# Layout of the count indicators, shorter vector steps in two routing phases, and the routing's rank, in a chunked attention and two-stage expert kernel

## The chip, the cores and the metric
The program runs on one core of a Trainium2 chip. The metric is the device time of one execution in microseconds. Before the change three runs took 1070.49, 1070.74 and 1074.46 us; the median is 1070.74 us. In the profile PE is TensorE's matmul, PEld its weight load, DVE is VectorE, ACT ScalarE, POOL GpSimd and SP the queue that issues most DMAs.

## The reference
Three stages follow each other, on 3072 tokens of 512 values.

```python
# 1 attention: chunks of 32 queries see 16 keys to the left, 8 to the right, and 8 memory keys
a = softmax(scale * q_c @ k_full.T);  x = a @ v_full
# 2 dense layer
r = maximum(x @ w_in, 0);  x = (s * r * r + b) @ w_out
# 3 experts: each token to one of 8 experts, at most 384 tokens each
order = argsort(-(x @ w_gate).flatten())
for idx in order:                 # all (token, expert) pairs, best first
    tok, e = idx // E, idx % E
    if assigned[tok] >= 0 or counts[e] >= cap: continue
    assigned[tok] = e;  counts[e] += 1
for e in range(E):
    out[mask_e] = maximum(x[mask_e] @ w1[e], 0) @ w2[e]
```

The loop over pairs can't be run pair by pair. It is computed in 8 phases. In each, every free token names its best open expert; the kernel searches the value at which the first expert would be full, accepts the tokens above it, and closes that expert. Which expert closes in a phase is known on the chip only, and its weights are then loaded by that number.

## The kernel before
**Stages.** Attention and the dense layer run over 24 tiles of 128 tokens, two tiles in a group. The dense products take each float32 operand as a rounded high part and a remainder, three matmuls for one. The last products of the dense layer (`late_products`, L366, matmuls `o` of L346) are kept back, so that TensorE has work while the first phase of routing runs. When the last of them is done, the last tile leaves PSUM (L373), is stored to DRAM, and the first expert's tokens are gathered from there (L994), transposed (`px`, L1014), split in high part and remainder (`xgh`, `xgl`, L1005 to L1010), and go through the two expert layers (`pf` in `ffn1`, `pg` in `ffn2`).

**A routing phase** (`route`, L810) makes five searches, of 7, 7, 6, 6 and 6 bits. A search compares each token's value with 128 or 64 thresholds: the indicators, 1 or 0, one column of thresholds for each of the 24 token tiles. They are bf16 and lie in two halves of 12 tiles each (`HT = 12`); the table of thresholds has 6 columns alike (`TB = 6`). VectorE makes a half in one step (`indicate`, L737; for the first search of the first phase in blocks, L726). TensorE then counts: 24 matmuls `pc` (L832), one for each token tile, with the tile's 128 indicators as weights and the 8 columns `oh` as the moving operand, after one matmul with constants. VectorE forms a minimum and maximum (`fl`, L835), TensorE spreads it (`pb`, L838), VectorE subtracts the threshold found (L843), and the next search begins. After five searches come sums (`pt`), the closed expert's number (`ei`), the list of its tokens (`listing`, L906, with `po` and `pi`), and the next phase.

Names in the trace: the indicators have no buffer of their own but stand in reused ones, so that they appear as `vw` (and sources as `kwin`, `wk`, `kT`). VectorE's routing instructions all carry L582, and matmuls of the planned part L761.

**Order of the work.** From the first phase on, the order of instructions on TensorE, VectorE and ScalarE is written by a planner (`run`, L776; `choose`, L767). It keeps a clock per engine from fixed prices (`Timed`, L567; 0.047 us for a `pc` matmul). Each task is a generator that yields an engine, a wait and a rank; among tasks ready on an engine, the lowest rank goes first, then the earliest. Between two yields a task's instructions stand together. The main work (late products, then experts) fills TensorE wherever no task is due. On the chip an engine runs its instructions in this order and waits for semaphores.

**Weights of the experts.** Each expert has two halves (h even: first layer, odd: second layer), each half four parts of 512 KB. A part is loaded by SP into a ring of four buffers, rounded by ScalarE (`rounding`, L964), and the remainder is formed by VectorE (`second`, L972, `e<-raws,e` in the trace). Ranks: routing 1 in phases 0 and 1, then 3; weight parts 1 for the first two halves, then 2.

Of the kernel before, what the change touches and what calls it, by code (L numbers as in the profile page):

```python
# [9 lines left out]
F32 = mybir.dt.float32  # L10
F32R = mybir.dt.float32r
BF16 = mybir.dt.bfloat16
I32 = mybir.dt.int32
AF = mybir.ActivationFunctionType
ALU = mybir.AluOpType
# [3 lines left out]
P = 128  # L19
# [5 lines left out]
def kernel(ctx, tc, q, k, v, mem_k, mem_v, w_in, w_out, moe_s, moe_b,  # L25
# [523 lines left out]
    RB = ((25, 7), (18, 7), (12, 6), (6, 6), (0, 6))  # L549
    NR = len(RB)  # L550
    T = NTILE
    NH = 2
    HT = T // NH
    TB = HT // 2
# [30 lines left out]
    V = Timed()  # L585
# [30 lines left out]
    sp = b0 = Pool()  # L616
# [22 lines left out]
    tabs, steps = [], []  # L639
    for r, (sh, nb) in enumerate(RB):  # L640
        n, lo = 2 ** nb, -2.0 ** 31 if r == 0 else 0.0
# [37 lines left out]
    def bt(x, n=T):  # L679
        return x[:, :, None].to_broadcast([P, x.shape[1], n])  # L680

    def be(x):
        return x[:, None, :].to_broadcast([P, E, T])
# [4 lines left out]
    def small(shape, dt, name):  # L688
        return sp.tile(shape, dt, tag=name, name=name)
# [1 line left out]
    ids, eid = {}, {}  # L691

    def indicators(n):
        return [sp.tile([P, P, HT], BF16, tag=f"ind{g}", name=f"ind{n}_{g}") for g in range(NH)]

    part = {}

    def prep(ph, t0, t1=T):

        n = t1 - t0  # L700
        if ph not in part:
            part[ph] = [small([P, E, T], F32, "Lm"), small([P, T], F32, "m"), small([P, T], I32, "sg"),
                        small([P, NR, T], I32, "di"), small([P, E, T], BF16, "eq"), small([P, T], BF16, "mw"),
                        small([P, E, T], BF16, "oh"), sp.tile([P, T], BF16, tag="de", name=f"de{ph}", bufs=2),
                        indicators(f"{ph}_0") if ph < E - 1 else None]
        Lm, m, sg, di, eq, mw, oh, de, ind = part[ph]
        Lz, mz, gz, dz, qz, wz, oz, ez = (x[..., t0:t1] for x in (Lm, m, sg, di, eq, mw, oh, de))

        def bn(x):
            return x[:, None, :].to_broadcast([P, E, n])  # L710

        V.tensor_tensor(Lz, L[:, :, t0:t1], bt(shut, n), op=ALU.add)
        V.tensor_reduce(mz, Lz.rearrange("p e t -> p t e"), axis=AX.X, op=ALU.max)
        yield
        V.tensor_tensor(qz, Lz, bn(mz), op=ALU.is_equal)
        V.tensor_tensor(qz, qz, bt(w8, n), op=ALU.mult)
        V.tensor_reduce(wz, qz.rearrange("p e t -> p t e"), axis=AX.X, op=ALU.max)
        V.tensor_tensor(oz, qz, bn(wz), op=ALU.is_equal)
        yield
        if ph < E - 1:  # L720
            mi = mz.bitcast(I32)
            V.tensor_scalar(gz, mi, 31, 2 ** 31 - 1, op0=ALU.arith_shift_right, op1=ALU.bitwise_and)
            V.tensor_tensor(gz, gz, mi, op=ALU.bitwise_xor)
            V.tensor_tensor(dz, gz[:, None, :].to_broadcast([P, NR, n]), masks[:, :, t0:t1], op=ALU.bitwise_and)
            V.tensor_tensor(ez, dz[:, 0, :], act[:, t0:t1], op=ALU.min)
            if ph == 0:  # L726
                for a in range(t0 - t0 % TB, t1, TB):
                    g, a, b = a // HT, max(a, t0), min(a + TB, t1)
                    V.tensor_tensor(ind[g][:, :2 ** RB[0][1], a - g * HT:b - g * HT],
                                    de[:, None, a:b].to_broadcast([P, 2 ** RB[0][1], b - a]),  # L730
                                    tabs[0][:, :, a % TB:a % TB + b - a], op=ALU.is_ge)
            for g in range(NH) if ph else ():
                if g:
                    yield
                indicate(ind[g], de, g, 0)

    def indicate(ind, de, g, r):  # L737
        n, z = 2 ** RB[r][1], [P, 2 ** RB[r][1], HT // TB, TB]
        V.tensor_tensor(ind[:, :n, :].rearrange("p n (a b) -> p n a b", b=TB),
                        de[:, g * HT:(g + 1) * HT].rearrange("p (a b) -> p a b", b=TB)[:, None].to_broadcast(z),  # L740
                        tabs[r][:, :, None, :].to_broadcast(z), op=ALU.is_ge)

# [2 lines left out]
    V_PE, PE_V, PE_A, A_V = 0.13, 0.19, 0.33, 0.06  # L747
# [11 lines left out]
    def matmul(cost, *args, **kw):  # L759
        clk["pe"] += cost  # L760
        return nc.tensor.matmul(*args, **kw)  # L761
# [45 lines left out]
    def slack(ph):  # L807
        return 0.1 if ph < 2 else 0.4

    def route(ph):  # L810

        rank = 1 if ph < 2 else 3
        sl = slack(ph)
        yield "v", 0.0, rank
        for _ in prep(ph, 0 if ph else T - GT):
# [1 line left out]
        oh, di, de, ind = (part[ph][i] for i in (6, 3, 7, 8))  # L819
        os = [small([P, E, T], BF16, f"os{i}") for i in range(2)]  # L820
        if ph < E - 1:
            for r in range(NR):
                ind = ind if r == 0 else indicators(f"{ph}_{r}")
                for g in range(NH) if r else ():
                    if g == NH // 2 and ph > 0:
                        yield "v", 0.0, rank
                    indicate(ind[g], de, g, r)
                yield "pe", V_PE - 0.5 + sl, 0
                pc = psa[0].tile([P, E], F32, tag="pa", name=f"pc{ph}_{r}")
                matmul(0.05, pc, first, q2, start=True, stop=False)  # L830
                for t in range(T):
                    matmul(0.047, pc, ind[t // HT][:, :, t % HT], oh[:, :, t], start=False, stop=(t == T - 1))  # L832
                yield "v", PE_V, 0
                fl = small([P, E], BF16, "fl")
                V.tensor_tensor_scan(fl, pc, ones[:, 0:E], 0.0, op0=ALU.max, op1=ALU.min)  # L835
                yield "pe", V_PE + sl / 2, 0
                pb = psa[0].tile([P, 2], F32, tag="pa", name=f"pb{ph}_{r}")
                matmul(0.05, pb, steps[r], fl[:, E - 2:E], start=True, stop=True)  # L838
                c = pb[:, 1:2]
                yield "v", PE_V, rank  # L840
                if r < NR - 1:
                    dn = sp.tile([P, T], BF16, tag="de", name=f"de{ph}_{r}", bufs=2)
                    V.scalar_tensor_tensor(dn, de, c, di[:, r + 1, :], op0=ALU.subtract, op1=ALU.add)  # L843
                    de = dn
            V.scalar_tensor_tensor(os[1], be(de), c, oh, op0=ALU.is_equal, op1=ALU.mult)
            pin = small([P, E, T], BF16, "pin")
            V.tensor_tensor_scan(flat(pin), flat(cont), flat(os[1]), 0.0, op0=ALU.mult, op1=ALU.add)
            V.scalar_tensor_tensor(os[0], be(de), c, oh, op0=ALU.is_gt, op1=ALU.mult)
            row = small([P, E], BF16, "row")
            with nc.allow_low_precision("counts of at most 24"):  # L850
                V.tensor_reduce(row, os[0], axis=AX.X, op=ALU.add)
            yield "pe", V_PE + sl, 0
            pt = psa[0].tile([P, 3 * E], F32, tag="pa", name=f"pt{ph}")
            matmul(0.05, pt[:, 0:E], ones, row, start=True, stop=True)
            matmul(0.05, pt[:, E:2 * E], ones, pin[:, :, T - 1], start=True, stop=True)
            matmul(0.05, pt[:, 2 * E:3 * E], tri, pin[:, :, T - 1], start=True, stop=True)
            yield "v", PE_V, rank
            need = small([P, E], F32, "need")
            V.tensor_tensor(need, rem, pt[:, 0:E], op=ALU.subtract)
            take = small([P, E], F32, "take")  # L860
            V.tensor_tensor(take, need, pt[:, E:2 * E], op=ALU.min)
            V.tensor_tensor(rem, need, take, op=ALU.subtract)
        else:
            V.scalar_tensor_tensor(os[0], be(act), 0.0, oh, op0=ALU.is_gt, op1=ALU.mult)
            V.memset(rem, 0.0)
# [21 lines left out]
        a = sp.tile([P, T], BF16, tag="a", name=f"a{ph}", bufs=2)  # L887
# [76 lines left out]
    def rounding(h):  # L964

        ph, half = divmod(h, 2)
        ws = [bigw([FT2, DM] if half else [KD, F2], f"e{half}{ph}_{a}") for a in range(2)]
        EW[ph] += ws
        rank = 1 if h < 2 else 2
        left = [NP]  # L970

        def second(hi, lo, raw):  # L972
            yield "v", A_V, rank
            V.tensor_tensor(lo, raw, hi.bitcast(F32), op=ALU.subtract)
            parted[0] += 1
            left[0] -= 1
            if not left[0]:
                loaded.add(h)

        for i in range(NP):  # L980
            while (h, i) not in raws:
                yield "a", 0.4, rank
            raw, at = raws[h, i]
            yield "a", 0.0 if h < 3 or i == 0 else 0.5, rank, at
            hi, lo = (w[part_of(h, i)] for w in ws)
            scalar(hi, raw, AF.Copy)
            new(second(hi, lo, raw), "a")
# [205 lines left out]
```

## Time and profile before
| | |
|---|---|
| median of three runs | 1070.74 us |
| the profiled execution | 1072.39 us |
| its span, first to last instruction | 1070.6 us |
| mean granted clock of TensorE | 0.984 |
| PE busy | 1010.0 us, 94% |
| DVE busy | 793.8 us, 74% |
| ACT busy | 460.7 us, 43% |
| POOL busy | 204.7 us, 19% |
| HBM read, written | 82.33 MB, 12.60 MB |

Busy times are sums over an engine's instructions; ends of matmuls are modelled and overlap, so the distance from one start to the next says more than a duration. [...] Routing and experts lie between about 683 us and the end.

### The profile page before, as it was taken

Reading aid. Unit: us, or ns where it says so; the run is one execution under the profiler, and the core shown is the slowest. Engines: PE = TensorE matmul, PEld = TensorE weight load, DVE = VectorE, ACT = ScalarE, POOL = GpSimd, SP = SyncE. Lnnn points to the kernel's source line nnn. Section 1 sums busy time; section 2 is a strip of 40 time slices with the busy share of each in tenths; the row PEclk is TensorE's granted clock in tenths of the full one; section 3 lists DMA queues with packets and bytes.
Section 4 is the critical chain, followed back from the end, with each engine's and each line's share of the span. In section 5 each row is a group of like instructions: output and inputs, shape, how many; then the busy total and the mean of one; then the engine's idle time right before and its main releaser. Section 6 shows DMA issues by size and latency. Waiting matters only on the chain.

```text
span 1070.6 us, 24583 instructions
## 1 busy us (share of the span) xinstructions
PE 1010.0 (94%) x9397; PEld 888.7 (83%) x9397; DVE 793.8 (74%) x2879; ACT 460.7 (43%) x991; POOL 204.7 (19%) x227
## 2 busy tenths in 40 slices
PE   4668899999999999999999999987999999999997
PEld 3647688888988889888888889866898988988996
DVE  4999864986698969898969854376968769678720
ACT  3666554444444544445444445312414334233621
POOL 2566540000021101021101000001103202032211
PEclk9989999999999999999999999996999999999999
DMA  6966504221212121212121100032624426235600
GB/s 158 230 184 185 148 19 128 58 58 38 58 38 59 39 58 38 57 39 59 38 58 39 38 2 2 20 117 91 197 92 145 130 88 208 88 140 176 227 30 30
DMA packets 140373, 96.52 MB, mean 90 GB/s; under 512 B 99288, under 2 KB 123864, under 8 KB 140128
## 3 DMA queue, kind: packets, MB, share of 16 engines
q1 hardware_dynamic: 135968, 81.32, 27.1%
q0 software_dynamic: 4000, 13.11, 3.4%
q8 instruction: 74, 1.21, 0.5%
q10 hardware_dynamic: 288, 0.52, 0.1%
q14 instruction: 43, 0.35, 0.1%
HBM read 82.33 MB, written 12.60 MB: 89 GB/s over the span
## 4 chain that ended last, share of the span: by engine, by line
PE 72%; DVE 14%; issue 6%; DMA 4%; ACT 1%; POOL 1%; SPq 1%; POOLq 0%; DVEq 0%; ACTq 0%
PE o L346 20%; PE ph L316 20%; PE pf L761 11%; PE pg L761 9%; DVE lsc L387 5%; PE pc L761 5%; DVE u L280 2%; DVE y L281 1%; DVE g L325 1%; PE po L221 1%; DMA xg<-x2d,vw 1%; PE sc L195 1%; PE px L1014 1%; DMA raw<-in_moe_w_out_dram 1%; DMA k<-in_k_dram 1%
## 5 line engine op out<-in xcount | busy, mean ns | idle before, releaser
L316 PE MATMUL ph<-xT,win 128*128 128x256 f32 x2304 | 321.9, 288 | 9.7 <-ACT win L262 6.9
L316 PEld LDWEIGHTS ph<-xT,win 128*128 128x128 f32 x2304 | 300.0, 192 | 27.5 <-ACT win L262 10.3
L346 PE MATMUL o<-wout,g 128*128 128x512 f32 x1038 | 275.3, 401 | 5.2 <-DVE g L325 2.2
L346 PEld LDWEIGHTS o<-wout,g 128*128 128x128 f32 x1038 | 185.1, 190 | 39.7 <-DVE g L325 3.1
L387 DVE SCALAR_TENSOR_TENSOR lsc<-x,wgb 128x128 int8<-128x128 f32 x640 | 158.2, 298 | 3.3 <-DMA wgb<-wgd 1.2
L320 ACT ACTIVATE r<-ph 128x256 f32<-128x256 f32 x192 | 72.7, 381 | 166.5 <-PE ph L316 155.8
L761 PE MATMUL pf<-xgh,e 128*128 128x384 f32 x512 | 137.9, 345 | 0.0
L761 PE MATMUL pg<-e,hh 128*128 128x512 f32 x384 | 124.3, 399 | 0.0
L325 DVE TENSOR_TENSOR g<-r,g 128x256 fp32r<-128x256 f32 x173 | 80.7, 468 | 53.3 <-ACT g L324 50.5
L387 DVE SCALAR_TENSOR_TENSOR lsc<-c,wgb 128x512 int8<-128x512 f32 x128 | 99.1, 774 | 2.1
L761 PEld LDWEIGHTS pf<-xgh,e 128*128 128x128 f32 x512 | 94.0, 192 | 0.4 <-ACT xgh L765 0.2
L761 PE MATMUL pf<-xgl,e 128*128 128x384 f32 x256 | 88.3, 345 | 0.3 <-DVE xgl L582 0.3
L765 ACT ACTIVATE hh<-pf 128x384 fp32r<-128x384 f32 x64 | 31.5, 492 | 129.1 <-PE pf L761 87.0
L765 ACT ACTIVATE e<-raws 128x1024 fp32r<-128x1024 f32 x64 | 65.7, 1056 | 45.5 <-DMA raws<-in_moe_w_dram 45.4
L321 ACT ACTIVATE r<-r 128x256 f32<-128x256 f32 x192 | 79.6, 417 | 5.5
L761 PEld LDWEIGHTS pg<-e,hh 128*128 128x128 f32 x384 | 71.1, 189 | 12.5
L582 DVE TENSOR_TENSOR e<-raws,e 128x1024 fp32r<-128x1024 f32 x64 | 76.8, 1218 | 3.9 <-ACT e L765 3.0
L761 PE MATMUL pg<-e,hl 128*128 128x512 f32 x192 | 75.8, 395 | 0.0
L324 ACT ACTIVATE g<-r 128x256 fp32r<-128x256 f32 x173 | 71.7, 417 | 5.0 <-PE o L346 0.3
L994 POOL DMA_INDIRECT xg<-x2d,vw x24 | 34.8, 1451 | 151.8 <-issue 118.2
L761 PE MATMUL pc<-kwin,vw 128*128 128x8 bf16 x840 | 56.2, 204 | 7.3 <-DVE vw L582 7.3
L582 DVE SCALAR_TENSOR_TENSOR hl<-pf,hh 128x384 fp32r<-128x384 f32 x64 | 35.1, 551 | 35.6 <-ACT hh L765 35.6
(171 smaller groups left out, 1276.7 us busy)
## 6 DMA issues: line engine op xcount, KB each, us to landing
raws<-in_moe_w_dram SPq DMA_DIRECT2D x64, 512.0 KB
vw<-in_v_dram SPq DMA_DIRECT2D x176, 56.0 KB
raw<-in_moe_w_in_dram SPq DMA_DIRECT2D x16, 512.0 KB
raw<-in_moe_w_out_dram SPq DMA_DIRECT2D x16, 512.0 KB
k<-in_k_dram SPq DMA_DIRECT2D x24, 256.0 KB
q<-in_q_dram SPq DMA_DIRECT2D x24, 256.0 KB
x2d<-x SPq DMA_DIRECT2D x20, 256.0 KB
wgb<-wgd SPq DMA_DIRECT2D x1, 2048.0 KB
```

Source lines behind the costliest of these rows:

```text
L280: nc.vector.scalar_tensor_tensor(u, yi, 3, u, op0=ALU.logical_shift_left, op1=ALU.bitwise_or)
L316: nc.tensor.matmul(ph, win_ap(a, kk, f), x[:, kk, :], start=(n == 0), stop=(n == 3 * KD - 1))
L320: nc.scalar.activation(r, ph, AF.Relu)
L321: nc.scalar.activation(r, r, AF.Square)
L324: nc.scalar.activation(hi, r, AF.Copy)
L325: nc.vector.tensor_tensor(lo, r, hi.bitcast(F32), op=ALU.subtract)
L346: nc.tensor.matmul(PO[j][u], g[:, u * P:(u + 1) * P], wout_ap(a, f), start=(f == 0 and n == 0), stop=(f == FT - 1 and n == 2))
L387: nc.vector.scalar_tensor_tensor(sc[:, z], a[:, z], 1.0, b[:, z], op0=ALU.mult, op1=ALU.mult, accum_out=acc[:, i:i + 1])
L582: return getattr(nc.vector, name)(out, *args, **kw)
L761: return nc.tensor.matmul(*args, **kw)
L765: nc.scalar.activation(out, in_, func)
L994: nc.gpsimd.indirect_dma_start(out=xg[:, j, :], out_offset=None, in_=x2d[:, :], in_offset=bass.IndirectOffsetOnAxis(ap=ids[ph][:, j:j + 1] ...
```

## The change
The change edits four places.

1. The indicators' layout. Each half is now two blocks of six token tiles; in a block the thresholds are the outer and the six tiles the inner index. Neighbouring thresholds of one tile stand 6 elements apart instead of 12. `indicate` writes both blocks of a half in one step as before, with the axes in the new order.
2. In phases 0 and 1 the indicators are made block by block (768 or 384 elements a step, no longer 1536 or 768); in the first search of phase 1 the planner may put other work between the blocks.
3. `second` forms the remainder of a weight part in two steps for the first three halves, and other work may come between.
4. Routing has rank 2 instead of 3 from phase 2 on, the same as weight parts.

```diff
     def indicators(n):
-        return [sp.tile([P, P, HT], BF16, tag=f"ind{g}", name=f"ind{n}_{g}") for g in range(NH)]
+        return [sp.tile([P, HT // TB, P * TB], BF16, tag=f"ind{g}", name=f"ind{n}_{g}")
+                .rearrange("p k (n b) -> p k n b", b=TB) for g in range(NH)]
...
-            if ph == 0:
-                for a in range(t0 - t0 % TB, t1, TB):
-                    g, a, b = a // HT, max(a, t0), min(a + TB, t1)
-                    V.tensor_tensor(ind[g][:, :2 ** RB[0][1], a - g * HT:b - g * HT],
-                                    de[:, None, a:b].to_broadcast([P, 2 ** RB[0][1], b - a]),
-                                    tabs[0][:, :, a % TB:a % TB + b - a], op=ALU.is_ge)
-            for g in range(NH) if ph else ():
+            for a in range(t0 - t0 % TB, t1, TB) if ph < 2 else ():
+                if ph and a:
+                    yield
+                a, b = max(a, t0), min(a - a % TB + TB, t1)
+                V.tensor_tensor(ind[a // HT][:, a % HT // TB, :2 ** RB[0][1], a % TB:a % TB + b - a],
+                                de[:, None, a:b].to_broadcast([P, 2 ** RB[0][1], b - a]),
+                                tabs[0][:, :, a % TB:a % TB + b - a], op=ALU.is_ge)
+            for g in range(NH) if ph > 1 else ():
                 if g:
                     yield
                 indicate(ind[g], de, g, 0)
 
     def indicate(ind, de, g, r):
-        n, z = 2 ** RB[r][1], [P, 2 ** RB[r][1], HT // TB, TB]
-        V.tensor_tensor(ind[:, :n, :].rearrange("p n (a b) -> p n a b", b=TB),
-                        de[:, g * HT:(g + 1) * HT].rearrange("p (a b) -> p a b", b=TB)[:, None].to_broadcast(z),
-                        tabs[r][:, :, None, :].to_broadcast(z), op=ALU.is_ge)
+        n, k = 2 ** RB[r][1], HT // TB
+        z = [P, k, n, TB]
+        V.tensor_tensor(ind[:, :, :n, :],
+                        de[:, g * HT:(g + 1) * HT].rearrange("p (a b) -> p a b", b=TB)[:, :, None, :].to_broadcast(z),
+                        tabs[r][:, None, :, :].to_broadcast(z), op=ALU.is_ge)
...
-        rank = 1 if ph < 2 else 3
+        rank = 1 if ph < 2 else 2
...
-                    indicate(ind[g], de, g, r)
+                    if ph > 1:
+                        indicate(ind[g], de, g, r)
+                    else:
+                        n = 2 ** RB[r][1]
+                        for k in range(HT // TB):
+                            V.tensor_tensor(ind[g][:, k, :n, :], de[:, None, g * HT + k * TB:g * HT + (k + 1) * TB]
+                                            .to_broadcast([P, n, TB]), tabs[r], op=ALU.is_ge)
...
-                    matmul(0.047, pc, ind[t // HT][:, :, t % HT], oh[:, :, t], start=False, stop=(t == T - 1))
+                    matmul(0.047, pc, ind[t // HT][:, t % HT // TB, :, t % TB], oh[:, :, t], start=False, stop=(t == T - 1))
...
         def second(hi, lo, raw):
-            yield "v", A_V, rank
-            V.tensor_tensor(lo, raw, hi.bitcast(F32), op=ALU.subtract)
+            m = raw.shape[1]
+            k = m // 2 if h < 3 else m
+            for z in range(0, m, k):
+                yield "v", A_V if z == 0 else 0.0, rank
+                V.tensor_tensor(lo[:, z:z + k], raw[:, z:z + k], hi[:, z:z + k].bitcast(F32), op=ALU.subtract)
```

## Rows read from the trace of the kernel before
**Rows 1.** The page: engine, busy us (share of the span), instructions.
```profile
PE 1010.0 (94%) x9397; PEld 888.7 (83%) x9397; DVE 793.8 (74%) x2879; ACT 460.7 (43%) x991; POOL 204.7 (19%) x227
```
**Rows 2.** Windows: stretch, its us, busy us per engine (instructions), PEclk, DMA, GB/s.
```profile
685.00:715.00 30.00, 30.00 (x230) 23.95 (x229) 18.79 (x59) 2.12 (x2) 0.74 (x1) 1.00 0.27 90
710.00:745.00 35.00, 23.45 (x186) 19.91 (x184) 25.95 (x52) 10.61 (x13) 5.71 (x4) 0.66 0.44 145
860.00:903.60 43.60, 43.60 (x319) 38.55 (x318) 34.23 (x83) 15.31 (x24) 8.53 (x6) 1.00 0.40 135
745.00:1055.00 310.00, 309.92 (x2072) 276.41 (x2071) 220.08 (x512) 110.28 (x169) 56.68 (x43) 1.00 0.40 131
```
**Rows 3.** The chain of waits, expert layers without other work: start, us, what.
```profile
759.55 5.49 PE pg L761 x24
...
996.29 16.67 PE pf L761 x96
```
**Rows 4.** The tile `pc`, and two of its streams in the timeline.
```profile
L761 PE MATMUL pc<-kwin,vw x840: 188/204/232, 685.4 to 966.2; 128*128 128x8 bf16 x168
...
693.41 1.61 PE L761 MATMUL pc<-kwin,vw 128*128 128x8 bf16 x24
...
900.41 1.58 PE L761 MATMUL pc<-kwin,vw 128*128 128x8 bf16 x24
```
**Rows 5.** The timeline: first of three matmuls with contiguous bf16 weights, and their successor.
```profile
882.60 0.18 PE L761 MATMUL pt<-wk,kT 128*128 128x8 bf16 x1
...
882.69 0.42 PE L761 MATMUL pf<-xgl,e 128*128 128x384 f32 x1
```
**Rows 6.** Half a stream at the lower clock: its window and its matmuls.
```profile
723.75:724.75 1.00, 0.89 (x12) 0.80 (x12) 1.00 (x2) 0.84 (x1) 0.95 (x1) 0.50 1.06 320
...
723.81 0.89 PE L761 MATMUL pc<-kwin,vw 128*128 128x8 bf16 x12 [2.08 <-DVE vw L582]
```
**Rows 7.** VectorE's indicator steps: groups (busy us, mean ns), two in the timeline.
```profile
L582 DVE TENSOR_TENSOR vw<-vw,wk 128x1536 bf16<-128x1536 bf16 x8 | 7.5, 953 | 0.1
L582 DVE TENSOR_TENSOR vw<-vw,wk 128x768 bf16<-128x768 bf16 x14 | 7.3, 554 | 0.2
L582 DVE TENSOR_TENSOR vw<-kwin,kT 128x256 bf16<-128x256 bf16 x1 | 0.4, 402 | 0.0
692.60 1.02 DVE L582 TENSOR_TENSOR vw<-kwin,kT 128x768 bf16<-128x768 bf16 x2
```
**Rows 8.** The chain between second stage and first expert (first row: timeline).
```profile
716.64 0.96 DVE L582 TENSOR_TENSOR vw<-vw,kT 128x1536 bf16<-128x1536 bf16 x1
...
717.51 0.74 DVE x L373
...
723.80 7.66 DMA xg<-x2d,vw
...
732.62 1.45 PE pc L761 x25
...
734.41 0.88 ACT xgh L765 x2
...
735.33 1.94 DVE xgl L582 x4
...
738.08 1.63 PE pc L761 x24
```
**Rows 9.** Weight remainders (group), and the timeline before one expert's first layer.
```profile
L582 DVE TENSOR_TENSOR e<-raws,e 128x1024 fp32r<-128x1024 f32 x64 | 76.8, 1218 | 3.9 <-ACT e L765 3.0 <-PE pf L761 0.9
...
899.25 0.95 DVE L582 TENSOR_TENSOR vw<-vw,kT 128x1536 bf16<-128x1536 bf16 x1
900.12 1.22 DVE L582 TENSOR_TENSOR e<-raws,e 128x1024 fp32r<-128x1024 f32 x1
906.67 0.55 DVE L582 TENSOR_TENSOR xgl<-px,xgh 128x384 fp32r<-128x384 f32 x1
911.45 0.34 PE L761 MATMUL pf<-xgh,e 128*128 128x384 f32 x1
```

## Prediction
> **What bounds the kernel now.** I read the page first: TensorE is busy for 94% of the span, VectorE for 74% [rows 1]. A share alone does not say that TensorE is the limit, so I read the windows next [rows 2]: the reader is to see that from 745 to 1055 us TensorE is busy for 309.92 of 310.00 us, and for all of a stretch of 43.60 us, which is one expert with one phase of routing. Busy could still hide slow issue, so I looked at how the matmuls of an undisturbed expert follow each other: 96 of the first layer take 16.67 us, or 174 ns for 384 columns, and 24 of the second take 5.49 us, or 229 ns for 512 [rows 3]. Both are 0.45 ns per column, so the columns set the pace and not the issue, and these 33.1 us per expert stay. What is left of the 43.60 us is mostly counting: one count is a stream of 25 matmuls with 8 columns each, which holds TensorE for 1.45 us (one of them on the chain [rows 8]), five times per expert, 7.3 us or 17%.
>
> In this half of the kernel TensorE has real idle time only between 710 and 745 us, 35.00 - 23.45 = 11.55 us [rows 2]. There the chain of waits leaves TensorE: it runs through the step of VectorE that takes the second stage's last tile out of PSUM (717.51), its store, the gather (7.66 us of DMA), the transposes and the subtractions to the first expert [rows 8].
>
> **Term 1: the weight load of a count.** The tile loads 128 weights per matmul, bf16. Before, neighbouring weights stand 12 elements (24 bytes) apart; after, 6 elements (12 bytes). The number of matmuls stays: 7 phases of 5 searches over 24 tiles, 840 [rows 4]. In the stream that starts at 693.41, 24 matmuls take 1.61 us, the last alone 0.204 us, so one follows the other after (1.61 - 0.20)/23 = 61 ns; other streams give 60. Three matmuls of the same shape with contiguous weights, the group pt, begin at 882.60, and the next matmul at 882.69: 30 ns each [rows 5]. So the step costs a factor of two, though it is twelve times the contiguous one: it looks like a step in the cost and not a slope. [...]
>
> No row has weights 12 bytes apart. The bounds are the two rows: 60 ns (no gain) and 30 ns (all of it). A loss I exclude, because the step moves toward the cheap row. Twelve is 10 bytes from the contiguous row and 12 from the strided one; a line drawn between them would give 44 ns. Since the ratio of two looks like a threshold I take 35 ns, near the contiguous row, and keep 44 as a case of its own. Saving: 24 x (60 - 35) = 0.60 us per stream, at the ends 0 and 0.72.
>
> [...]
>
> How many streams lie on the path? Between 685 and 715 us TensorE never waits, since products of the second stage fill every gap (30.00 us of 30.00 [rows 2]); a shorter stream ends that stage sooner: 5. In the idle stretch the first two streams of the second phase run while the gather is awaited and gain nothing; the third, 1.45 us from 732.62, stands on the chain in front of the last transposes [rows 8]. From it on all do: 3 of the second phase, 25 of the five after it. 33 x 0.60 = 19.8 us. This needs that nothing else takes over. Per expert VectorE has 34.23 us of work, DMA 0.40 of its time [rows 2]; at 40.6 us per expert VectorE would be at 84%.
>
> **Term 2: short steps in the first two phases.** One indicator step becomes two. From two steps in a row (1.02 us for two of 554 ns, so a pitch of 0.47 us for 768 elements; 0.953 against 0.554 us for 1536 and 768) a step costs 0.52 ns per element and 0.07 us beside [rows 7]. Two steps more per search are 0.14 us; 4 searches of the first phase and 5 of the second, 1.3 us of VectorE. In the first phase VectorE is busy for 18.79 us of 30.00 [rows 2] and TensorE is full, so it is covered; were that cover gone it would cost 4 x 0.14 = 0.6 us. Inside a stream a block lasts 0.5 us against 0.2 for its six matmuls, but the stream starts when three blocks are done, as before. In the second phase TensorE once waits for such a step (the stream at 738.08 comes straight behind one [rows 8]); I take +0.5 us in all. In return the store of the last tile, which started at 717.51 behind an indicator step of 0.96 us begun at 716.64 [rows 8], meets a step of half that: -0.4 us (0 to -0.9).
>
> **Term 3: halved remainders of the first three weight halves.** 12 subtractions of 1.218 us [rows 9] become 24 of some 0.65, about 0.7 us more of VectorE in all, while TensorE waits for the gather. At 735.33 the four subtractions on the chain start behind one of them; their own input was ready near 734.9 [rows 8], so -0.4 us (0 to -0.4).
>
> **Term 4: the routing's rank.** From the third phase on a routing step no longer yields to a weight part, the earlier ready one goes first. No work is added. It is queued in VectorE's order before later weight parts; behind these wait the matmuls of the next expert, and on SP the load of the part four later, which needs the same buffer. How much room is there? In one expert the last part of the first layer's weights starts at 900.12 and lasts 1.22 us, the last remainder of the gathered rows at 906.67, and the layer starts at 911.45 [rows 9]. That leaves the weights 10.1 us and the gathered rows 4.2 us. Routing's long steps in that stretch are four of 0.95 us, one of them between two parts [rows 9]; even all four, 3.8 us, cost the weights nothing, and the routing gains what they lose. Because TensorE now reaches each point sooner while VectorE's order is made with an unchanged price per count, I add +1.0 us for short waits (0 to 4).
>
> **Sum.** -19.8 + 0.5 - 0.4 - 0.4 + 1.0 = -19.1 us. From the profiled execution (1072.39 us, span 1070.6) that is 1053.3; the median of the runs lies 1.65 us below that execution, so 1051.6. I forecast 1052; this case's own range is 1046 to 1057 (30 ns and no waits; 38 ns and 4 us of waits).
>
> **Rivals.**
> *No gain from the step (chance 0.18).* If the quick load depends on weights that lie side by side, any gap costs the same, the stream stays at 60 ns, and terms 2 to 4 leave -0.3 to +0.7: 1070. For it: the only fast row is contiguous, and the two levels of the cost may have their step anywhere between 2 and 24 bytes. Against it: nothing in the trace but that 12 lies midway. [...]
> *Part of the gain (0.13).* If the cost is a slope after all, the line between the two rows gives 44 ns, 0.38 us per stream and 33 x 0.38 = 12.7 us; with the other terms 1059. For it: no row excludes a slope. Against it: 24 bytes cost only twice what 2 cost. [...]
> *Slower (0.07).* The indicator step walks its axes in a new order. A step of another walk, 256 elements in pairs, took 402 ns [rows 7], (0.402 - 0.155, what 554 ns leave beside 768 elements)/256 = 0.96 ns per element against 0.52. If the new order falls to that rate, a step of 1536 takes 0.7 us longer and one of 768 0.35. The second half of each of the first two searches then comes after the stream needs it: for the stream at 900.41 [rows 4] the second step, begun at 899.25 [rows 9], would end near 901.6 instead of 900.2 and is wanted at 901.1; with the next search 0.7 us per phase in five phases. The routing grows by 4 x 0.7 + 6 x 0.35 = 4.9 us per phase, over the 4.2 us that the gathered rows have: 0.7 in six phases. With streams at 60 ns that is +7.7: 1078. It decides from a step of about 1.4 us. Against it: both orders have runs of 6 elements, and such steps run at 0.52 ns now.
>
> **From cases to numbers.** Forecast case 0.62. A change below 0.5% (5.4 us) cannot be told from none here. Faster: the forecast and the part gain, 0.75. Same: 0.18. Slower: 0.07. The range runs from 1045 (33 x 0.72 us, and no waits) to 1069, taking in the part gain and the near end of no gain.
>
> **What would show it.** A count's stream of 25 matmuls at about 0.9 us instead of 1.46; steps of VectorE at unchanged 0.95 and 0.55 us; two experts 40.6 us apart instead of 43.6; the stretch without TensorE work after the second stage beginning 3 us sooner and as long as before. A stream at 1.4 us would prove term 1, and with it the forecast, wrong. A stream at 0.9 with experts still 43 us apart would mean that VectorE's or the routing's chain had become the limit: then TensorE shows idle time before the first layer.

## The result and the profile after

The changed kernel takes 1058.76 us (three runs, 1058.63 to 1059.53), the kernel before 1070.74: 12.0 us less by these medians. The ratio of the runs is 0.9876 [0.9853, 0.9900], which would be 13.3 us: the kernel before varied from 1069.4 to 1075.2 us between executions, and beside run 5 below it stood 12.9 us higher. The forecast was 1052 and the range 1045 to 1069. The profiled execution took 1058.63 us, 13.8 less than the one of before (1072.39).

The page of the changed kernel, in the columns of [rows 1]: TensorE is 12.2 us less busy with the same number of instructions, VectorE does as much as before.

```profile
PE 997.8 (94%) x9397; PEld 876.6 (83%) x9397; DVE 793.6 (75%) x2909; ACT 460.4 (44%) x991; POOL 202.1 (19%) x227
```

The counts come first. These are the tile `pc`, a stream of it in the timeline (start, us; the matmul with constants stands apart), and two entries of the chain of waits with that matmul (start, us, what):

```profile
L764 PE MATMUL pc<-kwin,vw x840: 177/190/213, 685.5 to 950.7; 128*128 128x8 bf16 x168
```

```profile
700.27 1.27 PE L764 MATMUL pc<-kwin,vw 128*128 128x8 bf16 x24
```

```profile
700.39 1.15 PE pc L764 x25
...
726.08 1.11 PE pc L764 x25
```

The median duration of one `pc` went only from 204 to 190 ns [rows 4], but they overlap; what matters is the distance between starts. 24 matmuls took 1.61 us [rows 4] and take 1.27: (1.27 - 0.19)/23 = 47 ns from one to the next, by the chain (1.15 - 0.04)/24 = 46, where it was 60. A stream of 25 holds TensorE for 1.15 us instead of 1.46 (1.45 in [rows 8]). The second of the two entries lies in a stretch where the granted clock is 0.50, half of full speed, and takes no longer (1.11 us).

Windows of the changed kernel, in the columns of [rows 2]; the third and fourth stretch are one expert with one phase each, from the start of one expert's first count to that of the next:

```profile
685.00:715.00 30.00, 29.40 (x233) 22.89 (x231) 19.99 (x69) 2.20 (x3) 0.74 (x1) 1.00 0.28 95
710.00:745.00 35.00, 24.96 (x213) 22.41 (x212) 28.92 (x75) 11.49 (x16) 4.40 (x4) 0.76 0.42 139
845.32:887.60 42.28, 42.28 (x323) 37.23 (x321) 34.18 (x83) 15.92 (x24) 8.97 (x7) 1.00 0.41 136
887.60:929.39 41.79, 41.79 (x320) 36.67 (x319) 34.08 (x83) 14.54 (x23) 7.27 (x7) 1.00 0.42 140
735.00:745.00 10.00, 10.00 (x94) 9.36 (x93) 7.39 (x20) 1.61 (x4) 0.00 (x0) 0.98 0.01 2
```

An expert takes 42.28 and 41.79 us, on average 42.03 instead of 43.60 [rows 2]: 1.57 us less, which is 5 streams x 0.31 us. TensorE stays busy throughout, so nothing else has become the limit. The last row belongs to the idle stretch; the same ten microseconds of the kernel before read:

```profile
735.00:745.00 10.00, 9.25 (x71) 7.90 (x69) 5.63 (x14) 1.55 (x4) 0.00 (x0) 0.61 0.00 0
```

Its granted clock there was 0.61 and is 0.98. At 0.50 (731 to 735 us here) the first expert's matmuls follow each other after 0.32 us, at 1.00 after 0.174, and fewer of them fall into the low stretch now. TensorE is idle for less time ahead of it (25 of 35 us busy between 710 and 745, where it was 23.45); that this is the cause was not tried. Part of it is chance: in run 5, which is the same kernel, the granted clock between 715 and 745 us was 0.66, where it is 0.72 in this execution.

The way into the idle stretch, first in the timeline (idle time before an instruction in brackets, with what ended it), then in the chain of waits:

```profile
711.84 2.54 PE L346 MATMUL o<-wout,k 128*128 128x512 f32 x10
...
715.15 0.74 DVE L373 SCALAR_TENSOR_TENSOR x<-o,s_col,wsum 128x512 f32<-128x512 f32 x1
...
731.83 0.67 PE L764 MATMUL pf<-xgh,e 128*128 128x384 f32 x1
```

```profile
716.21 2.36 DMA x2d<-x
...
719.55 5.38 DMA xg<-x2d,vw
...
724.97 1.11 PE px L1026 x4
```

The second layer of the first expert, in the timeline of the kernel before and then of the changed one:

```profile
759.39 0.62 PE L761 MATMUL pg<-e,hh 128*128 128x512 f32 x2
```

```profile
753.31 0.63 PE L764 MATMUL pg<-e,hh 128*128 128x512 f32 x2
```

The late products end at 714.38, 1.4 us earlier than before (715.79). The step that takes the last tile out of PSUM starts 0.77 us later, at 715.15; before, 1.72 us lay between the two (it started at 717.51, [rows 8]). The gather is issued in three parts, and the two chains show different ones: 5.38 us here is the first part, 7.66 us in [rows 8] the second. From the start of the first part to the first transposes it is 5.4 us here (719.55 to 724.97), where it was 6.4 (721.96 to 728.36). The first expert's first matmul starts at 731.83 instead of 734.96, and its second layer at 753.31 instead of 759.39, 6.1 us earlier.

So the 13.8 us of the two profiled executions read as follows. Up to the first expert's second layer 6.3 us (6.1, and 0.2 because routing starts 0.2 us later in this execution): 8 streams of 0.31 are 2.5, the earlier last tile is 0.95, and some 3 us remain for the shorter gather and the shorter stretch at the low clock. An estimate from the starts above gives about 1 and 2 us; no run separates them, and in run 5 this second layer starts at 754.38, 1.1 us later in the same kernel. From there on 25 streams x 0.31 = 7.75 us; the traces differ by 7.6.

Indicator steps and halved weight remainders of VectorE (group, busy us, mean ns):

```profile
L582 DVE TENSOR_TENSOR vw<-vw,wk 128x1536 bf16<-128x1536 bf16 x6 | 5.7, 953 | 0.1
...
L582 DVE TENSOR_TENSOR e<-raws,e 128x512 fp32r<-128x512 f32 x24 | 15.7, 683 | 0.0
```

The new order of axes costs nothing: 953 ns, and 555 for the steps of 768 elements, as in [rows 7]. Half a remainder takes 683 ns.

### The profile page after: what moved, and what is told of

Read it like the earlier page. It is cut to its first block, busy times and chain, and to the rows that moved or that the text cites. A ratio compares the mean times of both kernels' runs of the same rounds, so it can differ in the third digit from the quotient of the medians.

```text
span 1056.9 us, 24615 instructions
## 1 busy us (share of the span) xinstructions
PE 997.8 (94%) x9397; PEld 876.6 (83%) x9397; DVE 793.6 (75%) x2909; ACT 460.4 (44%) x991; POOL 202.1 (19%) x227
## 4 chain that ended last, share of the span: by engine, by line
PE 72%; DVE 13%; issue 8%; DMA 4%; ACT 1%; POOL 1%; SPq 1%; POOLq 0%; DVEq 0%; ACTq 0%
PE ph L316 20%; PE o L346 20%; PE pf L764 12%; PE pg L764 9%; DVE lsc L387 5%; PE pc L764 4%; DVE u L280 2%; DMA raw<-in_moe_w_out_dram 1%; DVE g L325 1%; PE po L221 1%; DVE y L281 1%; PE sc L195 1%; PE px L1026 1%; DMA xg<-x2d,vw 1%; DVE u L278 1%
## 5 line engine op out<-in xcount | busy, mean ns | idle before, releaser
L582 DVE TENSOR_TENSOR e<-raws,e 128x1024 fp32r<-128x1024 f32 (+1 forms) x76 | 78.1, 1048 | 2.8 <-ACT e L768 1.9
L1006 POOL DMA_INDIRECT xg<-x2d,vw x24 | 30.7, 1278 | 141.9 <-issue 64.3
L1099 POOL DMA_INDIRECT out_dram<-qk,vw x24 | 29.7, 1237 | 132.9 <-ACT qk L768 119.7
```

The source lines that it names most:

```text
L582: return getattr(nc.vector, name)(out, *args, **kw)
L1006: nc.gpsimd.indirect_dma_start(out=xg[:, j, :], out_offset=None, in_=x2d[:, :], in_offset=bass.IndirectOffsetOnAxis(ap=ids[ph][:, j:j + 1] ...
L1099: st_ = nc.gpsimd.indirect_dma_start(out=out[:, :], out_offset=bass.IndirectOffsetOnAxis(ap=ids[ph][:, j:j + 1], axis=0), in_=o, in_offset ...
```

## The experiments

Theory A was that the distance of the weights carries the gain and that the other three edits add little. Its first rival, theory B, was that the gain comes from the order and from shorter waits, so from the other edits. A second question was the law of the weight cost: a slope, a need for weights side by side, or a count of 16-byte stretches. Runs 2 and 12 put edits into the kernel before; each of the others is the changed kernel with one edit, run 10 with two.

**1. The old layout under the rest of the change.**

```diff
-        return [sp.tile([P, HT // TB, P * TB], BF16, tag=f"ind{g}", name=f"ind{n}_{g}")
-                .rearrange("p k (n b) -> p k n b", b=TB) for g in range(NH)]
+        return [sp.tile([P, P, HT], BF16, tag=f"ind{g}", name=f"ind{n}_{g}")
+                .rearrange("p n (k b) -> p k n b", b=TB) for g in range(NH)]
```

> The changed kernel with the indicators' old layout (12 elements between neighbouring weights); short steps, halved remainders and rank stay. Theory A (the shorter count streams carry the gain: 0.31 us less in each of the 33 streams on the path, 10.2 us; the other edits give the remaining 2 to 3 us in front of the first expert): streams back at 1.46 us, time 1067 to 1069. Theory B (the gain is one of order and of shorter waits, the streams only shrink beside): near 1060.

Measured: 1069.11 us, ratio to before 0.9962 [0.995, 0.9975]. A stream is back at its old length, by the chain of this kernel:

```profile
701.11 1.46 PE pc L764 x25
```

Most of the gain is gone with the layout. What stays is 4.1 us (0.4%), where terms 2 to 4 were put at about nothing (a loss of 0.7 us).

**2. The layout alone**, put into the kernel before: long indicator steps, whole weight parts and rank 3 stay.

> The kernel before with the new layout alone (long steps, whole remainders, rank 3). Theory A: streams at 1.15 us, time 1060 to 1061, the stretch between the second stage and the first expert as in the kernel before. Theory B: 1067 or more.

Measured: 1060.46 us, 0.9887 [0.9859, 0.9915], with streams like those of the changed kernel:

```profile
699.00 1.15 PE pc L762 x25
```

The layout alone brings 12 us, nearly all that the whole change does. So the 4.1 us of run 1 and these do not add up by the runs: with the layout in place, the other three edits together are worth 1.1 to 1.7 us by the medians (1060.46 against 1059.39 in run 5 and 1058.76), with overlapping intervals. The traces show where each part lies. The first expert's second layer, in run 1 and then in run 2:

```profile
755.38 0.63 PE L764 MATMUL pg<-e,hh 128*128 128x512 f32 x2
```

```profile
756.90 0.63 PE L762 MATMUL pg<-e,hh 128*128 128x512 f32 x2
```

Against 759.39 in the kernel before, the other three edits alone bring it 4.0 us forward, the layout alone 2.5 (8 streams of 0.31), and both together 6.1. From this point to the end of the span it is 311.2 us in the kernel before, 312.0 in run 1, 302.9 in run 2 and 303.6 in the changed kernel: behind the first expert's start only the layout counts. The profiled execution of run 2 is 1.1 us above its median, and two executions of the changed kernel reach this point 1.1 us apart, so a microsecond or two in front of it cannot be divided further.

**3. Blocks of four token tiles**: weights 8 bytes apart.

```diff
-    TB = HT // 2
+    TB = HT // 3
```

> The changed kernel with blocks of four token tiles, so that neighbouring weights stand 4 elements (8 bytes) apart. Lines theory (the load pays for each stretch of 16 bytes that it touches: 60 ns at 24 bytes, three quarters of it at 12, half of it at 8): 30 ns per matmul, a stream of 0.76 us, 33 x 0.38 = 12.7 us less than the changed kernel, 1046. Slope theory (a straight line from 30 ns at 2 bytes to 60 at 24): 38 ns, a stream of 0.95 us, 6 to 7 us less, 1052. If VectorE's steps with runs of 4 elements are slower than 0.52 ns per element, part of it is lost to waits.

Measured: 1049.63 us, 0.9782 [0.9763, 0.9801]; measured again 1049.22, 0.9789 [0.9766, 0.9812] (run 11). The chain, and VectorE's long step:

```profile
698.79 0.82 PE pc L764 x25
```

```profile
L582 DVE TENSOR_TENSOR vw<-wk,kT 128x1536 bf16<-128x1536 bf16 x5 | 4.8, 950 | 0.0
```

A stream takes 0.82 us, (0.82 - 0.04)/24 = 32.5 ns per matmul, nearer to the 30 of the lines theory than to the 38 of the slope, and VectorE's step is as quick as with runs of six. 33 x 0.33 us = 10.9 us were to be had, and 9 to 10 came. This kernel is faster than the one before and the changed one.

**4. The law by itself** (one execution). At the end of the changed kernel stand eleven extra streams of 24 matmuls, whose weights lie 1, 2, 3, 4, 5, 6, 7, 8, 10, 12 and 16 elements apart:

```diff
+        lw3 = [lw[:, 0:s * P].rearrange("p (n b) -> p n b", b=s) for s in (1, 2, 3, 4, 5, 6, 7, 8, 10, 12, 16)]
+        for i in range(11):
+            for t in range(24):
+                matmul(0.047, lp[:, i, :], lw3[i][:, :, t % lw3[i].shape[2]], lx, start=(t == 0), stop=(t == 23))
```

> The changed kernel with streams of 24 matmuls of the count's shape added after the last expert, whose weights stand 1, 2, 3, 4, 5, 6, 7, 8, 10, 12 and 16 elements apart (their sums are not used). Distance between starts in ns. Lines theory: 30, 30, 30, 30, 38, 45, 52, 60, 60, 60, 60. Slope theory: 30, 33, 36, 38, 41, 44, 46, 49, 55, 60, 71. Pairs theory (only neighbours lying together load fast): 30, then 60 throughout, which 46 ns at 6 elements already speaks against.

The timeline, one row per distance in that order (the matmul that ends each stream is left out):

```profile
1048.99 0.76 PE L764 MATMUL lp<-lx,lw 128*128 128x8 bf16 x24
...
1049.83 0.74 PE L764 MATMUL lp<-lx,lw 128*128 128x8 bf16 x24
...
1050.65 0.77 PE L764 MATMUL lp<-lx,lw 128*128 128x8 bf16 x24
...
1051.50 0.94 PE L764 MATMUL lp<-lx,lw 128*128 128x8 bf16 x24
...
1052.62 1.09 PE L764 MATMUL lp<-lx,lw 128*128 128x8 bf16 x24
...
1054.00 1.24 PE L764 MATMUL lp<-lx,lw 128*128 128x8 bf16 x24
...
1055.53 1.40 PE L764 MATMUL lp<-lx,lw 128*128 128x8 bf16 x24
...
1057.21 1.57 PE L764 MATMUL lp<-lx,lw 128*128 128x8 bf16 x24
...
1059.07 1.51 PE L764 MATMUL lp<-lx,lw 128*128 128x8 bf16 x24
...
1060.87 1.57 PE L764 MATMUL lp<-lx,lw 128*128 128x8 bf16 x24
...
1062.72 1.62 PE L764 MATMUL lp<-lx,lw 128*128 128x8 bf16 x24
```

Less the last matmul (0.18 to 0.2 us) and divided by 23, one matmul follows another after 25, 25, 26, 33, 39, 46, 52, 59.5, 57, 59.5 and 61.5 ns. The granted clock was not the same throughout. Windows over the streams with 4 and with 5 elements, in the columns of [rows 2]:

```profile
1051.50:1052.30 0.80, 0.80 (x27) 0.80 (x26) 0.00 (x0) 0.00 (x0) 0.00 (x0) 1.00 0.84 323
1052.62:1053.57 0.95, 0.95 (x26) 0.95 (x26) 0.00 (x0) 0.00 (x0) 0.00 (x0) 0.50 0.00 0
```

The streams with 1 to 4 elements ran at 1.00, those from 5 on at 0.50; the matmul that ends a stream (two records in the timeline) took 0.37 us behind the first three, 0.47 behind 4 elements and 0.57 or 0.58 from 5 on. Where both levels were measured the cost is nearly the same: 6 elements take 46 ns here and 46 in the changed kernel at 1.00; 12 elements 59.5 here and 60 in the kernel before at 1.00, and 63 at 0.50 [rows 6]. At 5, 7, 8, 10 and 16 elements there is no stream at 1.00, and at 1 to 4 none at 0.50.

From 4 to 8 elements the cost rises from 33 to 59.5 ns, by some 6 to 7 with each element; from 8 elements, 16 bytes, it stays at 57 to 61.5; up to 3 elements it stays at 25 to 26. That is close to 60 ns times the distance as a share of 16 bytes (6 elements: 12/16 x 60 = 45, measured 46; 4 elements: 30, measured 33), with 25 ns as the least measured. The lines theory fits these numbers; what the load does with 16 bytes was not shown. Weights that need not lie side by side to be quick rule out the pairs, and the flat parts, up to 3 elements and from 8 on, rule out a straight line from 2 to 24 bytes.

**5. The changed kernel again**, beside the next three.

> The changed kernel itself, for the same chip as the three that follow: 1058 to 1060.

Measured: 1059.39 us, 0.9875 [0.9854, 0.9895].

**6. Rank 3 again.**

```diff
-        rank = 1 if ph < 2 else 2
+        rank = 1 if ph < 2 else 3
```

> The changed kernel with routing back at rank 3 from the third phase on. Theory A (routing is not on the path after the first expert begins; weight parts have 10 us of room): within 1 us of the changed kernel. Rival (the rank lets the routing keep up with the faster matmuls): 3 us or more slower, with TensorE waiting in front of an expert's first layer.

Measured: 1068.02 us, 0.9967 [0.9954, 0.998], 8.6 us slower than run 5. Theory A failed here, and the rival was right. The profile shows where: the later gathers slip. The first of the three gathers for the second to the fourth expert, in the timeline of GpSimd in run 5 and then in this run, where a scatter of results now goes ahead of the last one:

```profile
757.04 0.94 POOL L1006 DMA_INDIRECT xg<-x2d,vw  x1 [34.08 <-DVE kwin L582]
...
797.92 0.98 POOL L1006 DMA_INDIRECT xg<-x2d,vw  x1 [20.64 <-issue]
...
839.31 0.98 POOL L1006 DMA_INDIRECT xg<-x2d,vw  x1 [18.40 <-PE pf L764]
```

```profile
756.81 0.94 POOL L1006 DMA_INDIRECT xg<-x2d,vw  x1 [32.83 <-DVE kwin L582]
...
801.57 0.98 POOL L1006 DMA_INDIRECT xg<-x2d,vw  x1 [25.25 <-issue]
...
845.21 0.97 POOL L1099 DMA_INDIRECT out_dram<-qk,vw  x1 [27.07 <-DVE wk L582]
846.49 1.54 POOL L1006 DMA_INDIRECT xg<-x2d,vw  x1 [0.30 <-issue]
```

The second expert's gather starts at the same time, the third's 3.65 us later, the fourth's 7.18 us later, while TensorE does not lag: the second layer of the third expert starts at 838.70 in run 5 and at 838.12 here. In the chain of waits of this run VectorE's routing steps lead up to the scatter and the gather; then come the gather itself (its last part) and TensorE, whose wait stands in the view of waits between 855 and 870 us (who waited for whom: us in total, times, longest). After the two follow the window of TensorE, and the start of the fourth expert's second layer in run 5 and in this run:

```profile
850.58 7.63 DMA xg<-x2d,vw
```

```profile
PE px L1026 <- DMA xg<-x2d,vw: 3.3, 2, 3.0
```

```profile
855.00:870.00 15.00, 11.00 (x89) 9.54 (x89) 9.52 (x16) 5.63 (x9) 0.99 (x1) 0.89 0.28 104
```

```profile
880.75 0.63 PE L764 MATMUL pg<-e,hh 128*128 128x512 f32 x2
```

```profile
886.85 0.63 PE L764 MATMUL pg<-e,hh 128*128 128x512 f32 x2
```

TensorE is idle for 4.0 of these 15 us, and the granted clock is 0.89 in them. One expert thus takes 48.7 us instead of 42.1, 6.7 of the 7.4 us by which the two profiled executions differ. At rank 3 the routing, whose gathers start 44.8 and 44.9 us apart, falls behind TensorE, whose second layers start 41.8 and 42.1 us apart, until the rows are late. The edit changes only the order against tasks of rank 2, and those are weight parts.

**7. Whole weight parts**: the remainders of the first three halves in one step each.

```diff
-            k = m // 2 if h < 3 else m
+            k = m
```

> The changed kernel with undivided remainders of the first three weight halves. Theory A (the divided ones let the gathered rows' remainders and the gather's issue start earlier): the first expert begins 0.5 to 1.5 us later, and so the end. Rival (they only cost VectorE 0.7 us): 0.5 us faster or equal.

Measured: 1062.82 us, 0.9911 [0.9893, 0.9929], 3.4 us slower than run 5 by the medians (1.4 by the two profiled executions); the two intervals overlap at their ends, but every execution here is slower than every one of run 5. In the timeline TensorE waits for a subtraction of the first expert's rows, which stands behind a whole remainder:

```profile
730.40 1.22 DVE L582 TENSOR_TENSOR e<-raws,e 128x1024 fp32r<-128x1024 f32 x1
...
731.54 1.94 DVE L582 TENSOR_TENSOR xgl<-px,xgh 128x384 fp32r<-128x384 f32 x4
...
732.14 0.69 PE L764 MATMUL pf<-xgl,e 128*128 128x384 f32 x1 [2.01 <-DVE xgl L582]
```

**8. Long indicator steps** in the first two phases, as before.

> The changed kernel with long indicator steps in the first two phases, in the new layout. Theory A (short steps let the last tile leave PSUM sooner): the last tile's step starts up to 1 us later after the last product, the end 0.5 to 1.5 us later. Rival (they only add 1.3 us to VectorE in a stretch where it is the busiest engine): equal or up to 1 us faster.

Measured: 1058.91 us, 0.988 [0.9859, 0.99], the same as run 5. The short steps cost and bring nothing here.

**9. Blocks of three token tiles**: weights 6 bytes apart.

```diff
-    TB = HT // 2
+    TB = HT // 4
```

> The changed kernel with blocks of three token tiles: weights 3 elements (6 bytes) apart. By the ladder 26 ns per matmul, a stream of 0.66 us, 33 x 0.49 = 16 us less than the changed kernel, 1043, if VectorE's steps keep 0.52 ns per element. Rival: with runs of three elements VectorE falls to about 1 ns per element, the routing grows by 5 us per phase and TensorE waits for it: 1050 or more.

Measured: 1055.01 us, 0.9841 [0.9817, 0.9864]: slower than blocks of four by 5.6 us, though a stream is shorter again. The chain, VectorE's long step, a window of TensorE, and its longest wait in it:

```profile
699.69 0.67 PE pc L764 x25
```

```profile
L582 DVE TENSOR_TENSOR vw<-wk,kT 128x1536 bf16<-128x1536 bf16 x10 | 12.2, 1215 | 0.0
```

```profile
745.00:800.00 55.00, 51.84 (x395) 45.10 (x393) 46.91 (x125) 18.61 (x29) 7.30 (x6) 0.97 0.42 140
```

```profile
PE pc L764 <- DVE vw L582: 1.7, 1, 1.7
```

33 x 0.15 us = 5 us should have been won. But a step of 1536 elements in runs of three takes 1215 ns instead of 950, and TensorE is idle again after the idle stretch (3.16 us of these 55; 4.9 between 745 and 1040, where blocks of four have 0.5 between 745 and 1035). Of the 3.16 us, 1.7 go to a count that waits for its indicators. The expected 1043 rested on VectorE keeping its pace; the rival, 1050 or more, is what was measured. That these waits tell the whole difference is not shown.

**10 and 11. Blocks of four, with and without a planner's price that fits them.**

```diff
-                    matmul(0.047, pc, ...
+                    matmul(0.033, pc, ...
```

> Blocks of four token tiles with the planner's price of a count's matmul at 0.033 us, as measured, instead of 0.047. Theory A (TensorE's order is full anyway, the price shifts only where filling stands): within 1.5 us of the run with four tiles, 1048 to 1051. Rival (the wrong price makes TensorE wait): 2 us or more faster.

> The kernel with blocks of four token tiles again, for comparison on one chip: 1049 to 1050.

Measured: 1048.43 us, 0.9781 [0.9759, 0.9804] with the price, 1049.22 without. The price is worth 0.8 us at most, and the intervals overlap. 1048.43 us is the lowest median of all kernels here.

**12. The layout with rank 2**, in the kernel before.

> The kernel before with the new layout and with rank 2, but with long indicator steps and undivided remainders. Theory A' (rank 3 costs time only where the order of the first phases lets the routing reach the third expert too late; with the layout alone no wait was seen): within 1.5 us of the run with the layout alone, 1059 to 1061. Rival (rank 2 is worth 8 us wherever counts are short): 1052 to 1054.

Measured: 1062.70 us, 0.9909 [0.9893, 0.9925], against 0.9887 for the layout alone (run 2). Here rank 2 is no gain, if anything a small loss. So the 8.6 us of run 6 are not the rank's own worth: they appear only beside the short steps and halved parts. Against run 8 this kernel lacks only the halved remainders, and it is 3.1 us slower by the ratios (3.9 for run 7 against run 5): at rank 2 the halved remainders are worth 3 to 4 us with short steps and with long ones.

## Why the prediction was right, and where it was off

**What came.** The direction and the range were right. The forecast was not: 1058.76 lies outside the forecast case's own range of 1046 to 1057, and a stream takes 1.15 us where about 0.9 was to show it. What came is the case of part of the gain, which had a chance of 0.13; that the range took it in is what made it right.

**Term 1: right in kind, mis-sized.** The saving comes from the distance of a count's weights (run 2: 1.15 us a stream with the layout alone), all 33 streams are on the path (five per expert give 5 x 0.31 = 1.55 of the 1.57 us measured), and nothing took over behind them. The step that failed is the choice of 35 ns "near the contiguous row" between the bounds of 30 and 60: it is 46, so 0.31 us per stream and 10.2 us (33 x 0.31) instead of 0.60 and 19.8. I had read "twelve times the distance costs only twice" as a threshold with everything below it cheap. Run 4 shows a rise from 33 ns at 8 bytes to 59.5 at 16 and a flat part from there (57 to 61.5), and 12 bytes lie on the rise. The granted clock does not explain the cost of the wide step: it is 61 ns at 1.00 ([rows 4], in a stretch of [rows 2]) and 63 at 0.50 [rows 6].

**Term 2: off in details.** The short steps as such are worth nothing (run 8), neither +0.5 nor -0.4. In the two traces the last tile did leave PSUM 0.95 us sooner after the late products, at the far end of the bound that I gave. In run 8, with long steps, this gap is back at 1.71 us (713.50 to 715.21) and the time is the same, so the kernel's time does not hang on it.

**Term 3: mis-sized.** It was put at -0.4 us; undone it costs 3.4 us (1.4 by the profiled executions). I had counted only the remainder ahead of the four subtractions. VectorE's extra work was 1.8 us (24 of 683 ns for 12 of 1218) and not 0.7; 24 of the 0.65 us that I took would already have made it 1.0. Run 7 shows TensorE waiting 2.01 us for them, in a stretch where the granted clock is low (0.60 between 715 and 745 us).

**Term 4: the wrong question.** I looked for what rank 2 would cost the weights and found room, and that held: TensorE's waits after the first expert's start name no weight part. I did not ask what rank 3 would cost now that TensorE reaches each point 1.6 us per expert sooner. I had worked out that the gathered rows have 4.2 us to spare, in another expert of the kernel before; in run 6 the fourth expert's gather starts 7.18 us later than in run 5, and TensorE's longest wait for its rows is 3.0 us, which leaves a room of the same size. The layout alone shows no such loss at rank 3 (run 2), with long steps and whole parts. Which of the two edits lets routing fall behind at rank 3 stays open, as it was not tried.

**The idle stretch** was to begin 3 us sooner and last as long. It began 1.4 us sooner, 5 x 0.31 = 1.55 by the true price less the 0.2 by which routing started later, and was shorter as well.

**The rivals.** The part gain had the right number: 44 ns, 1059 against 1058.76. Its law was wrong, since the straight line would say 49 ns at 16 bytes and 35.5 at 6, where run 4 has 59.5 and 26. No gain is refuted by the stream of 1.15 us and by run 4, and slower is refuted for runs of six (953 ns). Its mechanism exists, though: with runs of three VectorE's step does grow to 1215 ns, and run 9 pays for it.

So 1058.76 lies 7 us above the forecast. Term 1 was 9.6 us too high, and 2.6 us came back. In the traces it came back ahead of the first expert's second layer, where run 1 shows the other three edits at 4.0 us and terms 2 to 4 had put a loss of 0.7; but by the runs the layout alone brought about 12 us too, and this part stays open. The lower end of the range, 1045, is not what its working gives: 1070.74 - 23.8 - 0.3 = 1046.6.

## What to carry to other kernels

In run 4 a matmul with 8 columns took 25 to 26 ns with bf16 weights up to 3 elements apart, 33 at 4, 46 at 6 and 57 to 61.5 from 8 on. Weights closer together paid in these runs, as long as the engine that writes them kept its pace with such short runs (VectorE's step of 1536 elements: 950 ns with runs of 4, 1215 with runs of 3): a distance of 4 elements gave 1049 us, 3 gave 1055 and 6 gave 1059. When two rows are all that is known of a cost, their ratio does not say where between them the rise lies; here the middle of the bounds would have been the better choice. When the engine on the path becomes quicker, look again at each chain that had a few microseconds to spare, and ask what the order of before would now cost, not only what the new one does.

## What was unexpected of the hardware

Even with contiguous weights a pair of load and matmul with 8 columns took 25 ns in run 4, and a distance of 3 elements costs hardly more (26 ns). The cost of the two wider steps that were measured at both levels hardly depends on the granted clock: a stream with weights 6 elements apart takes 1.15 us at 1.00 and 1.11 at 0.50, and 12 elements cost 60 and 59.5 to 63 ns per matmul. VectorE's bf16 comparison of 1536 elements takes 949 to 962 ns with inner runs of 4 or 6 elements and 1215 to 1224 with runs of 3.
